# Tap weights over 128 partitions, own places for q, paired taps, a two-term third step and a new instruction order in a gated FFT-convolution and MLP kernel

## The chip, the cores and the metric

One core of a Trainium2 chip. The metric is the device time of one execution in microseconds. Engines are named as in the profile: PE (TensorE) with its weight loads PEld, DVE (VectorE), ACT (ScalarE), POOL (GpSimd), SP (SyncE, which issues the transfers).

## The reference

Inputs are 2048 tokens x 640 channels in bf16. With x = A_q:

```python
g = sigmoid((x * gate_w).sum(-1, keepdims=True))
# branch a
k_shift = sum over t of 4 taps: k shifted by t tokens * shift_k[:, t]
kv = k_shift * v
y  = irfft(rfft(kv, 2S) * rfft(ssm_k, 2S))[:S] + kv * ssm_D      # causal convolution over 2048 tokens
a  = x * y
# branch b
h  = gelu(layernorm(x) @ w1)                 # 640 -> 640
x1 = x + shift_four_channel_groups(h, +1, -1, +2, -2 tokens) @ w2
b  = x1 + gelu(layernorm(x1) @ w3) @ w4      # 640 -> 1536 -> 640
out = g * a + (1 - g) * b
```

## The kernel before

Everything is one list of 778 small tasks (`build`), each on one engine, and one order written out by hand as numbers (`ORDER`, a letter after a number puts the task on ACT, DVE or POOL). Instructions are issued in that order, so each engine runs its part as an in-order queue; `place` goes through the order once with estimated durations to choose buffers and the number of filler matmuls (`t.fill`, L255), which run on zeros while PE would idle at the start. What waits for what comes from the tasks' reads and writes.

Tokens are held as 16 tiles of 128 (token = 32 n + 16 g + s, tile s). The work in stages:

- *Head.* Transfers of x (`ldx`), w1, w2 (`ldw2a`, `ldw2b`), the convolution kernel (`ldsk`), k and v. Sine tables (TRIG, BM). For each tile of x: statistics (`st1`, L577 to L581 on DVE, L585 and L586 on ACT), 1/sqrt by a power on POOL (`rs1`, L594 to L597), normalisation (`nm1`, L601 or L631), transposes (`tr1`) and their eviction (`ev1`).
- *Branch b, first half.* `w1` (L689, L693) with gelu `g1`, `w2` (L715), `x1` (L722, adds into x and sums), squares `sq`, then `ve2` and `st2` on POOL or DVE for the second layernorm, `nm2` and transposing transfers `dt2` (L808).
- *Taps.* For four groups of four tiles (kv3, kv2, kv1, kv0), on DVE alone: four multiplications by a tap's weights (`m3` to `m0`, L878) into VC, three additions (`a2` to `a0`, L882), and the product with v (`v`, L886). The weights are loaded as one row on one partition (`ldCJ`), re-ordered there by one copy on POOL (`cjp`, 1 x 2560), written to memory (`wCJ`) and read back to all partitions (`rCJ`).
- *Convolution* by a factored Fourier transform. First step: `s1h` (L911) for the kernel and `s1x` (L913) for kv, evicted to FS and written to FH and FXD. It needs the last tap group for its last four tiles. Second step in ten blocks m: `s2h`, `s2x` (L965) and their evictions `e2` (to XH). `pa` and `pb` (L980) form the four real products on DVE, 2 x 2048 elements. Third step `s3` (L993): four terms accumulate, 32 matmuls a block:

```python
terms = [(0, 0, 0), (1, 1, 64), (0, 1, 96), (1, 0, 96)]
for n, (a, b, col) in enumerate(terms):
    for j in range(4):
        for gp in range(2):   # one matmul each
```

  `e3` evicts to GS, `wG` writes GD, `rG` reads it back into GX (four buffers), `s4` (L1031) is the last step, one tile each.
- *Branch b, second half.* `w3` (L817) in four groups of twelve with gelu `g2` (L824), `w4` (L833, L842), `t2` (L850) adds to x. The last four tiles are LATE: their w4 is cut into 512 and 128 columns.
- *End.* q is loaded again in pairs of tiles (`ldq`, two buffers in QO). `yq` (L1037) forms g * q * y on DVE into one of four places in W4's tile. `ad` (L1064) adds (1 - g) * x into one of two output buffers, for LATE tiles `ax` (L1045) and `fo` (L1051) do it in parts. `st` stores two tiles, or one for LATE.

The gate is `gate` (PE), `gz`, `gtanh`, `gg`. `dfold` adds ssm_D to the kernel's first row.

Of the kernel before, what the change touches and what calls it, by code (L numbers as in the profile page):

```python
# [31 lines left out]
WARM, COLD, PART = 7.5, 1.6, 0.95  # L32
# [5 lines left out]
41 0 23 5 29 94v 6 7 9 3 19 11 17 4 25 1 2 31 32 15 18 8 10 63v 12 13 14 26 27 87v 61a 85a 64 62 95v 104v 65v 28 42 88  # L38
86 393 24 44 96 209 43 210 55a 66v 89v 67 395 56 68a 58a 53v 54 97v 34 90a 30 399 396v 400v 57v 91 397 40 394a 93a 98
59 99v 100v 92v 60v 101 103v 143 147 16 20p 33 149 398a 102a 77a 145 79v 21 45 150 80 391 71v 72 46 22 144 148 69v  # L40
392v 82v 74a 121 39 122 450 70 78 146 107a 73v 458 35 75 451v 401p 438 37 81v 76v 439a 151 83 113v 123 36 459a 38 456
152 457a 49 84v 108 114 454 452 115v 116 125 455a 453a 110v 129 117v 446 444 126 460 118v 403 404 405 124 127 447a 162
163 406 130 128 156 157 440 105a 441a 407 159 153 154 106 160 461 47 445a 402 131 158 109a 155 442 111 132 137 443a
112a 408 161 462 466 48 138 409 463a 448 134 135 468 215p 216 449 164 140 469a 467a 119 413 141 51 221p 165 470 410 50
411 120a 166 222 223v 464 465a 167 474 471a 173 475a 174 171 217a 480 168 476 187 191 481a 482 193 477a 172 473 192
188 412 414 218 483a 478 169 195 189 170 181 415 416 417 479a 472 418 419 421 422 182 178 179 485 196 194 190 486 423
488 219a 484 225a 489a 175 220 487a 492 176 493a 136 203 424 204 494 425 490 206 498 207 495a 200 201 491a 420 426 427
428 430 502 499a 226 177 504 224 505a 211 503a 506 500 227 496 501a 239 507a 133 497 228 240 508 142 429 184 185 139
247 431 432 433 434 435 436 248 233 510 512 511a 231 513a 243 259p 509 249 514 235 234 260 232 244 515a 518 245 265p
# [34 lines left out]
class Plan:  # L84
# [13 lines left out]
    def add(self, name, eng, dur, fn, r=(), w=(), use=(), acq=(), rel=(), roles=(), after=(), mode=None, nbytes=0):  # L98
# [3 lines left out]
        t.kept = None  # L102
        t.acq = [(a, 1, a == "U") if isinstance(a, str) else a for a in acq]
# [43 lines left out]
    def place(self, order):  # L147
# [6 lines left out]
        mode, bw, flying, self.kept = None, 0.0, [], None  # L154
        start, end = [None] * n, [None] * n
        for i in order:
# [24 lines left out]
            if t.bytes:  # L181
                flying.sort()
                if len(flying) >= IN_FLIGHT:
                    at = max(at, flying.pop(0))
                start[i] = at
                free[e] = at + t.dur
                bw = max(bw, at + t.dur)
                bw += t.bytes / (HEAD_RATE if bw < HEAD else DMA_RATE)
                end[i] = bw + DMA_FIXED
                flying.append(end[i])  # L190
            else:
                d = t.dur
                if e == "PE":
# [3 lines left out]
                    if at < WARM:  # L197
                        d *= COLD
                        if self.kept is not None:
                            t.fill = int(0.95 * (at - max(free[e], 0.8)) / FILL_US[0])  # L200
                    elif self.kept is not None:
                        t.fill = max(0, int((WARM - free[e]) / FILL_US[0])) + int(PART * (at - max(free[e], WARM)) / FILL_US[1])
# [7 lines left out]
                free[e] = end[i] = at + d  # L210
            for (o, p, k) in t.rel:
# [47 lines left out]
class Env:  # L259
# [19 lines left out]
        "HT": ("H", [P, 16, D], BF16),  # L279
        "GS": ("H", [P, 10240], BF16),  # L280
# [3 lines left out]
        "XH": ("J", [P, 2, 2, 2048], BF16),  # L284
        "xn": ("L", [P, 4, D], BF16),
# [8 lines left out]
    def __init__(self, ctx, tc):  # L294
# [11 lines left out]
        self.taken = 0  # L306
# [25 lines left out]
    def early(self, name, shape, dtype):  # L332

        if name not in self.made:
# [3 lines left out]
            self.taken += n + n % 2  # L338
            v = self["C0"][0:shape[0], a:a + n]
# [15 lines left out]
def build(env, nc, io):  # L355
    pl = Plan()
    add = pl.add
    for name, n in (("U", 8), ("xn", 4), ("hs", 2), ("x1nT0", 1), ("x1nT1", 1), ("h2", 2), ("FS", 2), ("FX", 5), ("XS", 2), ("HS", 2), ("PP", 2),
                    ("GX", 4), ("Q", 2), ("O", 2), ("V", 4)):
# [51 lines left out]
    add("ident", "POOL", 0.55, c_id, r=["iotb"], w=["ID"])  # L411
# [89 lines left out]
    def c_bm(t):  # L501
        for g in range(2):
# [7 lines left out]
    dma("ldCJ", 5120, lambda t: nc.sync.dma_start(out=env["VC"][0:1, 2, :, :].rearrange("p j d -> p (j d)"),  # L510
                                                  in_=io["sk"].rearrange("d j -> (d j)").unsqueeze(0)), w=["CJR"], roles=("VC",))
    add("cjp", {"POOL": 3.2, "ACT": 2.3}, 0, lambda t: copy(t, env["VC"][0:1, 3, :, :],
                                                            env["VC"][0:1, 2, :, :].rearrange("p a b -> p (a b)").rearrange("p (d j) -> p j d", j=4)),
        r=["CJR"], w=["CJP"], roles=("VC",))
    dma("wCJ", 5120, lambda t: nc.sync.dma_start(out=env.CD[:], in_=env["VC"][0:1, 3, :, :].rearrange("p j d -> p (j d)")), r=["CJP"], w=["CD"],
        roles=("VC",))
# [56 lines left out]
    def f_st1(t, s):  # L573
        x = env["x"][:, s, :]
        if t.on == "DVE":
# [4 lines left out]
            nc.vector.tensor_scalar(out=SS("VE")[:, s:s + 1], in0=MV()[:, s, 1:2], scalar1=1e-5, scalar2=None, op0=ALU.add)  # L580
            nc.vector.tensor_scalar(out=SS("SA")[:, s:s + 1], in0=MV()[:, s, 0:1], scalar1=-1.0, scalar2=None, op0=ALU.mult)  # L581
        else:

            m = SS("SA")[:, s:s + 1]
            nc.scalar.activation(out=env["JK"][:], in_=x, func=ACT.Copy, scale=float(-1.0 / D), accum_out=m)  # L585
            nc.scalar.activation(out=env["JK"][:], in_=x, func=ACT.Square, scale=1.0, bias=m, accum_out=SS("SB")[:, s:s + 1])  # L586
# [3 lines left out]
    def f_rs1(t, s):  # L590

        c = slice(s, s + 1)
        if st1[s].on == "ACT":
            nc.gpsimd.tensor_scalar(out=SS("VE")[:, c], in0=SS("SB")[:, c], scalar1=1.0 / D, scalar2=1e-5, op0=ALU.mult, op1=ALU.add)  # L594
        nc.gpsimd.tensor_tensor(out=SS("RS")[:, c], in0=SS("VE")[:, c], in1=env.sm("MH", [P, 2])[:, 0:1], op=ALU.pow)
        if nm1[s].on == "ACT":
            nc.gpsimd.tensor_scalar(out=SS("NB")[:, c], in0=SS("SA")[:, c], scalar1=SS("RS")[:, c], scalar2=None, op0=ALU.mult)  # L597
# [21 lines left out]
    for s0 in pairs:  # L619
        nm = []  # L620
        for s in (s0, s0 + 1):
            st1[s] = add(f"st1.{s}", {"DVE": 1.26, "ACT": 1.73}, 0, lambda t, s=s: f_st1(t, s), r=[("x", s, 0), ("x", s, 1)],
                         w=[("MV", s)])
            add(f"rs1.{s}", "POOL", 0.85, lambda t, s=s: f_rs1(t, s), r=[("MV", s), "c0"], w=[("RS", s)])
        for s in (s0, s0 + 1):
            def f_nm1(t, s=s):
# [3 lines left out]
                else:  # L630
                    nc.vector.tensor_scalar(out=env["xn"][:, t.buf["xn"][0], :], in0=env["x"][:, s, :], scalar1=SS("SA")[:, c],  # L631
# [475 lines left out]
```

## Time and profile before

| | |
|---|---|
| three runs | 224.68, 225.11, 225.39 us (median 225.11) |
| the profiled execution | 227.05 us, its span 225.3 us |
| busy share of the span | PE 94%, DVE 84%, ACT 69%, POOL 20% |
| transfers | 57.94 MB, mean 257 GB/s |
| granted PE clock | 1.000 |

The span is the time from the first to the last instruction. Busy shares are means over stages of different kinds, so the stages have to be read one by one. PE's busy time holds the fillers.

### The profile page before, as it was taken

What the parts mean: (1) busy time and instruction counts of PE and PEld (TensorE: products, weight loads), DVE (VectorE), ACT (ScalarE), POOL (GpSimd) and SP (SyncE); (2) the same over time, 40 slices, a digit from 0 to 9 for tenths busy, and PEclk for the clock granted to TensorE, in tenths of its full rate; (3) what the DMA queues carried; (4) which work ended last, traced back from release to release, by engine and by line L of the source; (5) the groups of instructions that cost most, each with busy time, mean ns of one, the idle gap of its engine ahead of it and who ended that gap; (6) DMA issues with size and microseconds to landing.
All of it is one profiled execution on the core that took longest, in us unless ns stands there. A gap on an engine that the chain in (4) does not pass through costs nothing.

```text
span 225.3 us, 5381 instructions
## 1 busy us (share of the span) xinstructions
PE 212.7 (94%) x2161; PEld 106.4 (47%) x2178; DVE 189.3 (84%) x281; ACT 154.4 (69%) x225; POOL 45.8 (20%) x86
## 2 busy tenths in 40 slices
PE   3999889899999999999999999999999999999992
PEld 1576454466444444345543433334444555555561
DVE  7998896999999999997469989899857426989984
ACT  6998969799988999889658988888675002225000
POOL 7481532436200009930710000000000000000000
PEclk9999999999999999999999999999999999999999
DMA  6999999999999998979899989999992596988624
GB/s 193 281 308 232 220 237 238 327 233 327 349 240 287 241 272 252 379 270 270 193 367 311 373 154 285 316 304 309 247 255 88 185 374 209 281 250 249 203 64 116
DMA packets 39503, 57.94 MB, mean 257 GB/s; under 512 B 15027, under 2 KB 30645, under 8 KB 39478
## 3 DMA queue, kind: packets, MB, share of 16 engines
q1 hardware_dynamic: 39158, 57.27, 89.9%
q10 hardware_dynamic: 320, 0.33, 0.5%
q8 instruction: 17, 0.28, 0.5%
q14 instruction: 8, 0.07, 0.1%
HBM read 35.56 MB, written 18.36 MB: 239 GB/s over the span
## 4 chain that ended last, share of the span: by engine, by line
PE 63%; DMA 17%; DVE 12%; SPq 3%; issue 2%; ACT 1%; DVEq 0%
PE PS L817 18%; PE PS L833 17%; PE PS L715 9%; DMA x<-in_A_q_dram 7%; PE PS L965 5%; DMA W<-in_B_w_dram 4%; PE PS L689 4%; PE PS L993 4%; DMA SK<-in_A_ssm_k_dram 3%; DVE VC L878 3%; DVE VC L882 3%; DMA QO<-in_A_q_dram 2%; SPq L382 2%; PE PS L911 2%; PE PS L1031 1%
## 5 line engine op out<-in xcount | busy, mean ns | idle before, releaser
L824 ACT ACTIVATE h2T<-PS 128x512 bf16<-128x512 f32 x48 | 27.9, 605 | 27.3 <-PE PS L817 26.9
L833 PE MATMUL PS<-W,h2T 128*128 128x512 bf16 (+3 forms) x306 | 39.8, 298 | 0.3
L387 ACT CAST FS<-PS 128x1024 bf16<-128x1024 f32 x37 | 36.0, 1021 | 5.4 <-PE PS L913 3.5
L817 PEld LDWEIGHTS <-W 128*128 128x128 bf16 (+1 forms) x300 | 22.1, 103 | 29.4 <-issue 8.4
L833 PEld LDWEIGHTS <-h2T 128*128 128x128 bf16 (+1 forms) x312 | 22.4, 100 | 18.5 <-issue 1.6
L387 ACT CAST XH<-PS 128x1024 bf16<-128x1024 f32 x26 | 25.5, 1020 | 7.5 <-PE PS L965 7.4
L817 PE MATMUL PS<-x1nT,W 128*128 128x512 bf16 x120 | 28.5, 380 | 0.0
L817 PE MATMUL PS<-XB,W 128*64 128x512 bf16 (+1 forms) x180 | 28.5, 380 | 0.0
L980 DVE TENSOR_TENSOR PP<-XH 128x2048 bf16<-128x2048 bf16 x20 | 23.6, 1219 | 3.1 <-ACT XH L387 2.8
L878 DVE TENSOR_TENSOR VC<-K,VC 128x2560 bf16<-128x2560 bf16 x16 | 23.7, 1490 | 2.3 <-DMA W<-in_B_w_dram 2.1
L715 PE MATMUL PS<-W,hsT 128*128 128x128 bf16 (+1 forms) x155 | 23.5, 297 | 0.9 <-DMA W<-in_B_w_dram 0.6
L850 DVE TENSOR_TENSOR x<-PS,x 128x640 bf16<-128x640 f32 x12 | 9.8, 823 | 13.4 <-PE PS L833 13.2
L689 PE MATMUL PS<-xnT,W 128*128 128x512 bf16 x80 | 19.2, 379 | 0.1
L715 PEld LDWEIGHTS <-hsT 128*128 128x128 bf16 x160 | 12.8, 98 | 13.0 <-issue 1.1
L882 DVE TENSOR_TENSOR VC<-VC 128x2560 bf16<-128x2560 bf16 x12 | 17.9, 1489 | 0.3
L389 DVE CAST XH<-PS 128x1024 bf16<-128x1024 f32 x14 | 16.9, 1220 | 1.2 <-PE PS L965 1.1
L1037 DVE SCALAR_TENSOR_TENSOR W<-PS,GG,QO 128x640 bf16<-128x640 f32 x16 | 13.6, 877 | 2.4 <-PE PS L1031 1.9
L387 ACT CAST GS<-PS 128x1024 bf16<-128x1024 f32 x12 | 12.0, 1016 | 3.9 <-PE PS L993 3.9
L255 PE MATMUL PS<-C 128*128 128x512 bf16 x34 | 9.9, 434 | 3.8 <-DVE C L506 3.7
L842 PE MATMUL PS<-W,h2T 128*64 128x512 bf16 (+1 forms) x192 | 13.4, 299 | 0.0
L722 DVE SCALAR_TENSOR_TENSOR x<-PS,x 128x640 bf16<-128x640 f32 x16 | 12.8, 815 | 0.1
L965 PE MATMUL PS<-FX,TRIG 64*32 64x512 bf16 x320 | 12.4, 381 | 0.3 <-ACT GS L387 0.3
(115 smaller groups left out, 294.0 us busy)
## 6 DMA issues: line engine op xcount, KB each, us to landing
FH<-FS SPq DMA_DIRECT2D x8, 640.0 KB, 6.3
FXD<-FS SPq DMA_DIRECT2D x8, 640.0 KB, 5.0
FX<-FH SPq DMA_DIRECT2D x10, 512.0 KB, 6.0
FX<-FXD SPq DMA_DIRECT2D x10, 512.0 KB, 5.3
GX<-GD SPq DMA_DIRECT2D x8, 640.0 KB, 5.9
W<-in_B_w_dram SPq DMA_DIRECT2D x2, 1920.0 KB, 11.9
GD<-GS SPq DMA_DIRECT2D x8, 480.0 KB, 4.0
SK<-in_A_ssm_k_dram SPq DMA_DIRECT2D x5, 512.0 KB, 6.5
```

Of the source, the lines that this page charges most:

```text
L387: nc.scalar.copy(out=out, in_=in_)
L389: (nc.vector if t.on == "DVE" else nc.gpsimd).tensor_copy(out=out, in_=in_)
L689: nc.tensor.matmul(m[:, b, :], lhsT=W[:, 0, kb, 160 * fb:160 * fb + 128], rhs=rhs(kb, shifts[fb]), start=(kb == 0), stop=(kb == 4))
L715: nc.tensor.matmul(m[:, c0:c1], lhsT=env["hsT"][:, o.buf["hs"][0], fb, 128 * (s % 4):128 * (s % 4) + 128], rhs=env["W12"][:, 1, fb, c0:c1] ...
L817: nc.tensor.matmul(env.PS[q:q + w, t.buf["U"][0], :], lhsT=env["W3"][:, kb, 128 * fb + q:128 * fb + q + w], rhs=env.nT(int(nP[-1]))[:, :, ...
L824: nc.scalar.activation(out=env["h2T"][:, o.buf["h2"][0], fb, :], in_=env.PS[:, t.buf["U"][0], :], func=ACT.Gelu_apprx_tanh)
L833: nc.tensor.matmul(m[q:q + w, c0:c1], lhsT=env["h2T"][:, o.buf["h2"][0], fb, a:a + w], rhs=env["W4"][:, fb, c0:c1], start=(fb == 0), stop= ...
L878: nc.vector.tensor_tensor(out=VC[:, o], in0=env["K"][:, a + 3 - j:a + 7 - j, :], in1=w, op=ALU.mult)
L882: nc.vector.tensor_tensor(out=VC[:, 1], in0=VC[:, 1], in1=VC[:, 2], op=ALU.add)
L965: nc.tensor.matmul(env.U(t.buf["U"][0])[32 * j:32 * j + 32, gp, :], lhsT=CRI()[64 * gp:64 * gp + 64, 32 * pc:32 * pc + 32], rhs=X[64 * gp: ...
L980: nc.vector.tensor_tensor(out=env["PP"][:, o.buf["PP"][0], a, :].rearrange("p (b c) -> p b c", b=2), in0=X.unsqueeze(1).broadcast_to([P, 2 ...
L1037: nc.vector.scalar_tensor_tensor(out=u, in0=env.Uf(t.buf["U"][0])[:, 0:D], scalar=SS("GG")[:, s:s + 1], in1=env["QO"][:, 2 * q.buf["Q"][0] ...
```

## The change

- The tap weights are loaded as 128 partitions x 20 elements, re-ordered by one copy of that shape on DVE or ACT, and written to memory in runs of five elements; `rCJ` stays.
- Taps in pairs: one multiplication forms two taps (5120 elements) from overlapping rows of K; an addition of 5120, one of 2560, and the product with v follow. A group has five DVE instructions and not eight.
- `pa` and `pb` become one product of 4096 elements; a new task `pc` combines the products (one subtraction, one addition, 1024 elements each, DVE). Third step: two terms, 16 matmuls a block.
- Each pair of q tiles has a place of its own (five in QO, three in XH's tile, the latter after the last product). `yq` writes in place. New: `ox` on ACT scales x by (1 - g) in place, 16 of them. `ad` and `ax` become plain additions, `ad` on DVE or POOL, into x; stores read x.
- `st1` on DVE loses its last two small instructions; `rs1` on POOL always has one more. `st2` keeps only the power; its other two POOL instructions become one on DVE (`nb2`).
- `dfold`'s and `bperm`'s engines change by the order (DVE, ACT). Some early tables live in VC's tile.
- The order is new: 790 tasks. `place` knows transfers in parts, a warm-up of PE, and times in which POOL and DVE exclude each other. In the new order w2 stands 16th in SP's queue and was 22nd; x1.0 to x1.3, gz and nb2 of the first group stand ahead of taps they stood behind; all stores stand behind the last `rG`; seven `ad` are on POOL.

```diff
-    dma("ldCJ", 5120, lambda t: nc.sync.dma_start(out=env["VC"][0:1, 2, :, :].rearrange("p j d -> p (j d)"),
-                                                  in_=io["sk"].rearrange("d j -> (d j)").unsqueeze(0)), w=["CJR"], roles=("VC",))
...
+    dma("ldCJ", 5120, lambda t: nc.sync.dma_start(out=CJ()[:, 0:20], in_=io["sk"].rearrange("(p a) j -> p (a j)", a=5)), w=["CJR"], roles=("VC",))
+    add("cjp", {"DVE": 0.12, "ACT": 0.25}, 0, lambda t: copy(t, CJ()[:, 20:40].rearrange("p (j a) -> p j a", j=4), CJ()[:, 0:20].rearrange("p (a j) -> p j a", j=4)),
...
+        def taps(t, j, a=a, E=E):
+            VC, k = env["VC"], env["K"][:, a + 3 - j:a + 7 - j, :]
+            k = bass.AP(tensor=k.tensor, offset=k.offset, ap=[list(k.ap[0]), [-D, 2], [D, 4], [1, D]])
+            nc.vector.tensor_tensor(out=VC[:, 1:3] if j else E(), in0=k, in1=VC[:, 3, j:j + 2, :].unsqueeze(2).broadcast_to([P, 2, 4, D]), op=ALU.mult)
...
+        def comb(t, pa=pa):
+            PP = env["PP"][:, pa.buf["PP"][0]].rearrange("p a (b c) -> p a b c", b=2)
+            v = nc.vector if t.on == "DVE" else nc.gpsimd
+            for b, op in enumerate((ALU.subtract, ALU.add)):
+                v.tensor_tensor(out=PP[:, 0, b, :], in0=PP[:, 0, b, :], in1=PP[:, 1, 1 - b, :], op=op)
...
-            terms = [(0, 0, 0), (1, 1, 64), (0, 1, 96), (1, 0, 96)]
-            for n, (a, b, col) in enumerate(terms):
+            for n, col in enumerate((0, 96)):
...
+            def ox(t_, s=s):
+                nc.scalar.activation(out=env["x"][:, s, :], in_=env["x"][:, s, :], func=ACT.Copy, scale=SS("OG")[:, s:s + 1])
...
+            def ad(t_, s=s, i=i, u=Q):
+                x = env["x"][:, s, :]
+                (nc.vector if t_.on == "DVE" else nc.gpsimd).tensor_tensor(out=x, in0=x, in1=u(i), op=ALU.add)
```

More of the change, by code (lines that the diff above doesn't have):

```diff
@@ L116, in add @@
         return t
-    def close(self):
+    LOCKS = ("nm1.", "nm2.", "kv", "pa.", "pb.", "pc.", "ad.", "ax.", "bperm")
+    XFER = (("ldx10", 2, 0.55, 1.6), ("ldx6", 2, 0.55, 1.6), ("ldx", 2, 0.55, 0.66), ("ldkh1", 1, 0.45, 0.9), ("ldkh0", 2, 0.6, 0.6),
+            ("ldk", 2, 0.55, 1.4), ("ldv", 2, 0.55, 1.4), ("ldsk", 1, 0.45, 2.0), ("ldw1", 1, 0.45, 2.9), ("ldw2a", 1, 0.4, 1.9),
+            ("ldw2b", 1, 0.4, 0.25), ("ldw3", 1, 0.6, 5.3), ("ldw4", 1, 0.6, 5.3), ("bm", 2, 0.55, 1.5), ("rCJ", 1, 0.4, 1.9), ("ldCJ", 1, 0.4, 0.3), ("wCJ", 1, 0.4, 1.2),
+            ("wF", 1, 0.65, 1.8), ("rF", 1, 0.42, 1.4), ("rG", 1, 0.45, 1.75), ("dbt", 1, 2.4, 3.0), ("dt", 1, 1.3, 1.1), ("ldq", 2, 0.58, 0.68),
+            ("st.", 2, 0.6, 0.68))
+    def close(self):
+        for t in self.tasks:
+            if t.bytes:
+                q = next((x for x in self.XFER if t.name.startswith(x[0])), ("", 1, 0.4, max(0.1, t.bytes / 365e3)))
+                n, us = (1, 0.4) if t.name.startswith("st.") and t.bytes < 250000 else (q[1], q[3])
+                t.parts = [(q[2], us)] * n
+        for t in self.tasks:
+            t.lock, t.hold = t.name.startswith(self.LOCKS), t.name in ("cjp", "dfold", "bz") or t.name[:3] == "ad."
+            t.steps = {"rs": 1, "ve": 2, "st": 0}.get(t.name[:2], 0)
+            t.gelu = t.name.startswith(("g1.", "g2."))
         by_role = {}
@@ L181, in place @@
             if t.bytes:
-                flying.sort()
-                if len(flying) >= IN_FLIGHT:
+                for k, (issue, us) in enumerate(t.parts):
                     at = max(at, flying.pop(0))
[L185 to L190, printed above, removed]
-            else:
-                d = t.dur
+                    if k == 0:
+                        start[i] = at
+                    at += issue
+                    bw = max(bw, at) + us
+                    flying.append(bw + DMA_FIXED)
+                free[e], end[i] = at, bw + DMA_FIXED
+            else:
+                if t.lock and e == "DVE" and held[0] <= at < held[1]:
+                    start[i] = at = held[1]
+                more = 0.0
+                if e == "POOL" and at < locked[1]:
+                    if at >= locked[0]:
+                        start[i] = at = locked[1]
+                        more = 1.5 * t.steps if locked[2] else 0.0
+                    elif t.hold and at + t.dur > locked[0]:
+                        more = 3.0
+                        free["DVE"] += 3.0
+                d = t.dur + more
                 if e == "PE":
@@ L210, in place @@
                 free[e] = end[i] = at + d
+                if t.gelu and not gelu:
+                    gelu = True
+                    free[e] = end[i] = at + d + TABLE
+                if t.hold and e == "POOL":
+                    held = (at, end[i])
+                if t.lock and e == "DVE":
+                    locked = (at, end[i], t.name[:2] == "kv")
             for (o, p, k) in t.rel:
@@ L999, in ev3 @@
                 copy(t_, env["GS"][:, a:a + 1024], env.Uf(t.buf["U"][2 * h]))
[L1000 removed]
+            add(f"e3.{m}.{h}", {"ACT": 1.03, "DVE": 1.23}, 0, ev3, use=[t], rel=[(t, "U", 2 * h), (t, "U", 2 * h + 1)], w=[("GS", m % 5, h)], after=("HT", "EH"), roles=("GS",))
         i = m % 5
```

218 lines of the change are left out of this document (99 added, 119 removed), and 5 rows, old and new, of the table ORDER.

## Prediction

> **What bounds the kernel now.** I read the page first, then busy time by stretch with the cuts at turns of the chain of waits, then the waits of TensorE and VectorE, then the chain.
>
> ```profile
> span 225.3 us, 5381 instructions
> PE 212.7 (94%) x2161; PEld 106.4 (47%) x2178; DVE 189.3 (84%) x281; ACT 154.4 (69%) x225; POOL 45.8 (20%) x86
> ...
> 0.00:40.63 40.63, 33.71 (x287) 19.17 (x291) 34.58 (x98) 35.10 (x53) 18.77 (x44) 1.00 0.94 248
> 40.63:101.33 60.70, 60.16 (x434) 29.10 (x442) 59.44 (x72) 53.55 (x81) 22.02 (x27) 1.00 1.01 287
> 101.33:114.47 13.14, 13.09 (x103) 7.36 (x112) 7.17 (x16) 9.18 (x19) 5.01 (x15) 1.00 0.97 251
> 114.47:174.00 59.53, 58.94 (x831) 23.79 (x834) 51.96 (x50) 48.62 (x61) 0.00 (x0) 1.00 0.96 271
> 174.00:187.08 13.08, 12.97 (x95) 7.32 (x98) 4.43 (x5) 1.01 (x1) 0.00 (x0) 1.00 0.78 287
> 187.08:220.87 33.79, 33.78 (x426) 19.68 (x424) 30.66 (x40) 6.94 (x12) 0.00 (x0) 1.00 0.68 197
> 220.87:225.30 4.43, 0.00 (x0) 0.00 (x0) 1.05 (x3) 0.00 (x0) 0.00 (x0) 1.00 0.54 148
> ...
> L255 PE MATMUL PS<-C 128*128 128x512 bf16 x34 | 9.9, 434 | 3.8 <-DVE C L506 3.7
> ...
> 30.95 9.63 DMA W<-in_B_w_dram
> ...
> 96.30 1.49 DVE K L886
> ...
> 99.67 1.23 DVE FS L389
> ...
> 100.93 0.39 PE PS L913 x2
> 101.33 6.84 PE PS L833 x49
> ```
>
> In the stretch rows the columns are the length, then busy time of PE, weight loads, DVE, ACT and POOL, then clock, DMA share, GB/s. Two things stand there. From 40.63 to 220.87 TensorE is idle for 180.24 - 178.94 = 1.3 us, so every TensorE microsecond removed there can count. And before 40.63 it does little: 33.71 us less 9.9 us of fillers (L255), 23.8 of 40.63 us, so 16.8 us are lost, until w2 lands. But between 40.63 and 101.33 VectorE is as full (59.44 of 60.70), and the chain runs through it: the last tap group's product (L886) ends at 97.79, and only then come the last first-step products (L913), which end at 101.33. So the first 101 us have two bounds, TensorE and VectorE's queue of taps; the rest has one, TensorE. Only 4.43 us follow its last matmul.
>
> The execution in the profile took 227.05 us, 1.75 more than its span; the runs have a median of 225.11. I forecast the change of the span and apply it to that median.
>
> **Head and taps.** The new order puts w2's main load at place 16 of SP's queue, where it was 22nd, after x, w1 and two of five ssm_k blocks. Ahead of it and with it go about 5.3 MB instead of 9.4. At the first stretch's 248 GB/s 9.4 MB are 37.9 us, and it landed at 40.58, 2.7 later; 5.3 MB give 21.4 + 2.7 = 24 us. TensorE then finds first-layer and second-layer work some 10 us earlier, and a good part of the 16.8 lost us can go. That doesn't shorten anything by itself: the last first-step products still wait for the last tap group, so VectorE's queue up to there has to be counted.
>
> ```profile
> L878 DVE TENSOR_TENSOR VC<-K,VC 128x2560 bf16<-128x2560 bf16 x16 | 23.7, 1490 | 2.3 <-DMA W<-in_B_w_dram 2.1
> L980 DVE TENSOR_TENSOR PP<-XH 128x2048 bf16<-128x2048 bf16 x20 | 23.6, 1219 | 3.1 <-ACT XH L387 2.8
> ...
> 58.00 1.49 DVE L878 TENSOR_TENSOR VC<-K,VC 128x2560 bf16<-128x2560 bf16 x1
> 59.52 1.49 DVE L882 TENSOR_TENSOR VC<-VC 128x2560 bf16<-128x2560 bf16 x1
> ...
> L581 DVE TENSOR_SCALAR SA<-MV 128x1 f32<-128x1 f32 x10 | 1.4, 144 | 0.0
> L722 DVE SCALAR_TENSOR_TENSOR x<-PS,x 128x640 bf16<-128x640 f32 x16 | 12.8, 815 | 0.1
> L603 DVE TENSOR_SCALAR xn<-x,r,SB 128x640 bf16<-128x640 bf16 x10 | 4.3, 437 | 0.4 <-POOL SB L787 0.4
> ...
> 99.31 0.09 DVE xn L603
> ...
> 51.23 1.36 PE PS L715 x10
> ...
> L389 DVE COPY xnT<-PS 128x1280 bf16<-128x1280 bf16 (+2 forms) x6 | 4.1, 702 | 0.1
> ```
>
> L878 and L980 are the same operation at 2560 and 2048 elements: 271 ns for 512 more, 0.529 ns an element. A pair of taps (5120) then takes 1490 + 1355 = 2845 ns. A group goes from 8 instructions at a pitch of 1.52 us (59.52 less 58.00), 12.2 us, to three of 2.88 and two of 1.52, 11.7 us; four groups save 2.0. Two 144 ns instructions leave each of 10 statistics: at most 2.9, and since short ones overlap I take 1.3. x1.14 and x1.15 go behind the taps: 2 x 0.815, 1.6. What comes ahead of the last tap: one eviction more (the FS cast above, 1.23), three normalisations more (3 x 0.437 = 1.3), one eviction of xnT (0.7), gz (from 97.79 to 99.31, 1.5), and dfold, cjp and two small nb2, about 0.6. Sum 5.3 against 4.9: 0.4 us more, before waits. The taps stand at position 56 of VectorE's queue, not 44, so x1.0 to x1.3 are ahead of them and they wait for w2's landing too; w2 at 24 us is in time, if ScalarE's activations are. I take VectorE's idle time there as it was: the last product ends at 98.2. After it TensorE has five first-step products; w2.12 (1.36 us, the L715 row), which stood among them, is earlier now; I count 1.1 of it, since the products also wait for evictions. 101.33 + 0.4 - 1.1 is 100.6, **0.7 us earlier**. The ends: 4.5 us earlier still if most of VectorE's waits of the first 40 us go (40.63 - 34.58 = 6.0), 7 later if first-layer work arrives late.
>
> The tap weights themselves: ldCJ, wCJ and rCJ are SP's as before; the re-ordering copy is 128 lanes x 20 elements on VectorE, counted above. wCJ waits for it in SP's queue with ldsk4, ldk15 and rCJ behind; x1.0 is ahead of that copy, so these loads can't be issued before about 29 us. The taps want them at about 44, after 15 us, and ldk's landings take 9.5 us:
>
> ```profile
> K<-in_A_k_dram SPq DMA_DIRECT2D x8, 320.0 KB, 9.5
> ```
>
> I cost it at nothing; if that cover goes, the taps slip one for one. The Trainium skill, "DMA: Bandwidth & Descriptors" (Specifications), says that transfers below 512 B miss line rate by a read-modify-write, and wCJ now writes runs of 10 B; no row before prices that, and by it the slip would be part of the 7 us above.
>
> **Step three.** Two of four terms are dropped, and VectorE combines the products.
>
> ```profile
> L993 PE MATMUL PS<-PP,TRIG 32*64 32x512 bf16 x320 | 10.5, 379 | 0.1
> ...
> 173.00 1.00 PE PS L993 x32
> ...
> L389 DVE CAST XH<-PS 128x1024 bf16<-128x1024 f32 x14 | 16.9, 1220 | 1.2 <-PE PS L965 1.1
> L387 ACT CAST XH<-PS 128x1024 bf16<-128x1024 f32 x26 | 25.5, 1020 | 7.5 <-PE PS L965 7.4
> L601 ACT ACTIVATE xn<-x,NB,RS 128x640 bf16<-128x640 bf16 x4 | 3.6, 916 | 0.0
> ...
> 187.81 2.16 PE PS L817 x20
> ```
>
> 32 matmuls take 1.00 us; 16 take 0.50; ten times: **5.0 us less on TensorE**. VectorE: one product of 4096 elements is 1219 + 1084 = 2.30 us in place of 2.44, and two combining instructions of 1024 are 0.68 each, 1.35: 1.2 more per block, 12.1 in all. Does that fit? In 114.47:174.00 TensorE spends 59.53; minus 5.0, plus two more w4 (3.3 each; they come before the last third step in the new order; two are 6.84 in the chain's row at 101.33) and two w3.3 (1.1 each, two are 2.16) gives 63.3. VectorE: 51.96 + 12.1, two evictions less (2.4), three t2 more (2.4, as L722), 1.1 less in small things: 63.0. ScalarE: 48.62 + 2 evictions (2.0) + four ox (3.7, by the 916 ns row) + two nm2 (1.8): 56.1. So VectorE, which had 7.6 us of slack, has none: 63.0 against 63.3. Before, with slack, TensorE lost 0.59 there. Bounds for the new stalls: 0, and 5 (the whole saving). I take 1.5, nearer to the old 0.59.
>
> **End.** Each q block has a place of its own, so q loads no longer wait for buffers, and sums go in place into x.
>
> ```profile
> 163.56 12.25 SPq L1005 DMA_DIRECT2D GD<-GS  x5
> 178.80 9.37 SPq L1019 DMA_DIRECT2D GX<-GD  x5
> ...
> 187.08 0.73 PE L1031 MATMUL PS<-GX,BT 128*64 128x512 bf16 x8
> ...
> GX<-GD SPq DMA_DIRECT2D x8, 640.0 KB, 5.9
> ...
> L1064 DVE SCALAR_TENSOR_TENSOR QO<-x,OG,W 128x640 bf16<-128x640 bf16 x12 | 10.0, 878 | 0.3 <-DMA out_dram<-QO 0.3
> L865 POOL TENSOR_TENSOR HT<-HT,C 1x640 bf16<-1x640 bf16 x1 | 1.4, 1415 | 0.4 <-DVE HT L389 0.4
> ```
>
> From the last third step (174.00) to the first G load's issue are 4.8 us, to its landing 10.7. The old order covers that with four w4, 13.1 us; the new with two w4 and four w3.3, 10.9. That leaves 0.2, and s4.10 has 4.6 us between its buffer's release and its use against a landing of 5.9: I add 0.2 for both, 2 as the upper bound. The sums: sixteen scaled additions of 0.88 become plain ones of 1219 - 1408 x 0.529 = 0.47, nine of them on VectorE and seven on GpSimd, where the one comparable row (640 elements) has 1.4; ScalarE gets sixteen ox of 0.92, and it was busy 6.94 of the last 33.79 us. So VectorE gains some 10 us there (16 x 0.88 less 9 x 0.47) and TensorE stays the bound; the wait for q was beside it. The last addition now follows a 128-column piece with another store already issued: VectorE ended 1.05 us after TensorE, it will end about 0.4 after: **0.65 less**.
>
> GpSimd's additions meet VectorE:
>
> ```profile
> 57.56 0.19 POOL L775 TENSOR_TENSOR v<-S 128x2 f32<-128x2 f32 x1
> ...
> 88.68 1.54 POOL L775 TENSOR_TENSOR v<-S 128x2 f32<-128x2 f32 x1
> ```
>
> The same instruction takes 0.19 us between taps and 1.54, a tap's length, beside one. Longer pairs make such waits up to 2.85; they sit on statistics needed much later, 0 us. The Trainium skill, "SBUF — State Buffer" (Who interferes with whom), has it as an exclusive lock: whichever starts first keeps the other out for a whole instruction. By that rule, the trace agrees for GpSimd's side; its other side, VectorE held by an addition, speaks against the change and is a rival below.
>
> Sum: -0.7 - 5.0 + 1.5 + 0.2 - 0.65 = -4.65; 225.11 - 4.65 = **220.5 us**.
>
> **Rivals.** *The head pays too.* VectorE's early waits shrink by 4.5: 216.0. For: w2 at 24 us; 16.8 lost us. Against: 56 tasks ahead of the taps, about 40 us long by their rows. 0.18. *The saving turns into VectorE's bound*: in-order queues with 63.0 against 63.3 lose 3 more: 223.5. For: no slack; against: 0.59 lost so far. 0.17. The same with 4.5 lost is no change, 225.0: 0.06. *GpSimd holds VectorE*: seven additions of 1.4, each after waiting for a VectorE instruction of 0.9, are 16 us in a queue; st.8 waits for the last, and st.14 and st.12 stand behind it on SP: 1.5 later, 222.0. Against: the last G products for it come 10 us before TensorE's end. 0.05. *Slower: taps late.* If w2.0 to w2.3 or the tap weights arrive so that the first pair starts at 52 instead of 44, the last product ends at 106, everything behind slips by 8: 228.5. It decides from 4.7 us of slip on. For: four x1 and the re-ordering copy now stand ahead of the taps; against: DMA lead of 15 us. 0.14. The forecast keeps 0.40.
>
> **Numbers.** A measurement here tells about 0.3% (0.7 us) from no change. Faster: 0.40 + 0.18 + 0.17 + 0.05 = 0.80; same 0.06; slower 0.14. The range takes the head's case with 1.5 below it and the balance case with 2.5 above: 214.5 to 226.0; left out is most of the slower case and the far end of the first.
>
> **What would show it.** w2 landing near 24 us; first pair near 44, 2.85 each; the last L886-like product near 98; third steps of 0.50; TensorE idle by 1 to 3 us in the two-term stretch with VectorE over 95% there; no q wait at the end; 3.8 us behind the last matmul. A first pair after 49 makes the forecast wrong upward, a last product before 95 downward.

## Result and the profile after

The changed kernel takes 232.44 us (median of 4, 232.26 to 234.47) against 225.25 (224.68 to 225.71): a ratio of 1.034, 95% interval 1.028 to 1.040. It is 7.2 us slower where 4.65 less was forecast. Executions more than 1.5% above the fastest of their kernel are left out of all ratios below (two of four with four terms back and two of four with the fillers, which have no ratio for that), and the one profile that was taken in such an execution, with the sums on GpSimd again, isn't read. Times below are medians of all executions, except where two single times are named; ratios are to the kernel before, run beside each experiment on the same chip. A stretch or a wait is from the one execution in the profile.

The page of the kernel after, and its busy time by stretch, cut at the same turns as in the prediction (length, busy PE, weight loads, DVE, ACT, POOL, then clock, DMA share, GB/s):

```profile
span 230.8 us, 5076 instructions
PE 214.4 (93%) x2018; PEld 105.1 (46%) x2018; DVE 187.5 (81%) x253; ACT 168.9 (73%) x244; POOL 48.8 (21%) x91
...
0.00:47.47 47.47, 41.95 (x348) 23.79 (x349) 35.77 (x93) 39.89 (x64) 19.90 (x63) 1.00 0.83 217
47.47:104.07 56.60, 53.65 (x385) 24.96 (x384) 55.91 (x52) 45.30 (x68) 15.85 (x14) 1.00 1.00 291
...
117.17:184.71 67.54, 65.70 (x742) 26.07 (x742) 61.86 (x58) 56.34 (x71) 0.00 (x0) 1.00 0.90 257
184.71:195.61 10.90, 10.90 (x90) 5.92 (x90) 2.87 (x3) 3.31 (x5) 0.00 (x0) 1.00 0.83 266
195.61:226.92 31.31, 29.15 (x366) 17.09 (x362) 25.28 (x33) 12.09 (x19) 10.23 (x7) 0.95 0.71 209
226.92:230.80 3.88, 0.00 (x0) 0.00 (x0) 0.35 (x1) 0.00 (x0) 0.00 (x0) 1.00 0.54 141
```

TensorE still has its 214 us of work (212.7 before), but over a longer span. Against the prediction's own steps: first tap pair at 47.47 (forecast 44), end of the first step 104.07 (100.6), two-term stretch 67.54 (63.3 + 1.5), last third step to last matmul 42.21 (38.3: 13.08 + 33.79 - 8.8 + 0.2), behind it 3.88 (3.8). The three large misses are +3.5, +2.7 and +3.9. Each has lines of its own.

First miss: the chain of waits ahead of the taps (start, length, what; pieces under 0.1 us are left out, but for the copy VC), what VectorE waited for there, and the transfers in that time:

```profile
28.32 0.83 DVE x L737 x2
29.15 0.09 DVE VC L405
29.27 4.13 DMA CD<-VC
33.41 0.33 SPq L532
33.79 0.72 SPq L398
34.56 12.83 DMA K<-in_A_k_dram
...
38.88 1.22 DVE L405 COPY HT<-PS 128x2048 bf16<-128x2048 bf16 x1 [2.17 <-PE PS L875]
...
47.47 2.83 DVE L898 TENSOR_TENSOR VC<-K,VC 128x5120 bf16<-128x5120 bf16 x1 [3.20 <-DMA K<-in_A_k_dram]
```

```profile
28.90:34.60 5.70, 5.70 (x72) 4.66 (x71) 5.19 (x15) 4.43 (x11) 2.36 (x8) 1.00 0.38 27
```

The re-ordering copy of the tap weights (VC) stands behind x1.0 on VectorE; wCJ, the store of the copy, waits for it in SP's queue; rCJ, which reads it back, waits 4.13 us for the store; and two blocks of k (ldk11, ldk7) stand behind rCJ. From 28.9 to 34.6 the transfers move 27 GB/s. Part of that is the queue that stands still; but ldsk4 and ldk15 went out between 29.69 and 31.37 and hardly moved either, and why isn't shown. Then four loads of k go out at once, and what the first pair needs lands after 12.83 us. VectorE sits idle for it for 3.20 us: it is done with the instruction ahead of the pair at 44.27, where the forecast has the pair at 44.

Second miss: TensorE's groups of the third step (L993, now L1020) and of the second (L965, now L987), before and then after, and one third step from the chain after:

```profile
L993 PE MATMUL PS<-PP,TRIG 32*64 32x512 bf16 x320 | 10.5, 379 | 0.1
L965 PE MATMUL PS<-FX,TRIG 64*32 64x512 bf16 x320 | 12.4, 381 | 0.3 <-ACT GS L387 0.3
...
L1020 PE MATMUL PS<-PP,TRIG 32*64 32x512 bf16 x160 | 7.2, 387 | 0.3 <-DVE XH L405 0.2
L987 PE MATMUL PS<-FX,TRIG 64*32 64x512 bf16 x320 | 13.1, 382 | 1.3 <-ACT GS L403 0.5 <-DMA FX<-FH 0.3 <-DVE XH L405 0.2
...
126.00 0.57 PE PS L1020 x16
```

Half the matmuls of the third step (160 for 320) bring 10.5 us of busy time down to 7.2, not to 5.3.

Third miss, TensorE's waits, and the stretches behind the longest of them:

```profile
PE PS L1060 <- DMA GX<-GD: 2.2, 1, 2.2
```

```profile
209.80:212.00 2.20, 2.16 (x38) 1.71 (x40) 1.66 (x2) 1.05 (x2) 0.00 (x0) 0.71 0.18 70
212.00:214.00 2.00, 2.00 (x14) 0.84 (x12) 1.83 (x4) 0.00 (x0) 0.79 (x1) 0.50 0.02 4
214.00:216.00 2.00, 2.00 (x22) 1.10 (x20) 1.96 (x3) 0.00 (x0) 2.00 (x2) 0.97 0.04 10
```

Before block 10's fourth step TensorE waits 2.2 us for its G load, and right behind it the granted clock is 0.71, 0.50, 0.97. What the clock withholds there is 2.20 x 0.29 + 2.00 x 0.50 + 2.00 x 0.03 = 1.7 us.

### The profile page after: what moved, and what is told of

Read it like the earlier page. It is cut to its first block, busy times and chain, and to the rows that moved or that the text cites. A ratio compares the mean times of both kernels' runs of the same rounds, so it can differ in the third digit from the quotient of the medians.

```text
span 230.8 us, 5076 instructions
## 1 busy us (share of the span) xinstructions
PE 214.4 (93%) x2018; PEld 105.1 (46%) x2018; DVE 187.5 (81%) x253; ACT 168.9 (73%) x244; POOL 48.8 (21%) x91
## 4 chain that ended last, share of the span: by engine, by line
PE 36%; DVE 26%; DMA 21%; ACT 6%; issue 6%; SPq 3%; DVEq 0%; ACTq 0%
PE PS L833 10%; PE PS L849 9%; DVE VC L903 7%; PE PS L858 6%; DMA K<-in_A_k_dram 6%; DMA x<-in_A_q_dram 5%; DVE VC L898 4%; DVE x L737 4%; DMA FX<-FH 3%; DVE XH L405 3%; PE PS L730 3%; DMA GX<-GD 3%; DMA GD<-GS 3%; PE PS L987 2%; DVE PP L1002 2%
## 5 line engine op out<-in xcount | busy, mean ns | idle before, releaser
L403 ACT CAST FS<-PS 128x1024 bf16<-128x1024 f32 x37 | 35.6, 1024 | 7.9 <-PE PS L932 2.9
L840 ACT ACTIVATE h2T<-PS 128x512 bf16<-128x512 f32 x48 | 28.0, 608 | 12.9 <-PE PS L833 12.4
L1096 POOL TENSOR_TENSOR x<-x,QO 128x640 bf16<-128x640 bf16 x6 | 8.8, 1478 | 90.6 <-ACT x L1071 86.9
L403 ACT CAST XH<-PS 128x1024 bf16<-128x1024 f32 x23 | 22.9, 1020 | 5.0 <-PE PS L987 4.9
L730 PE MATMUL PS<-W,hsT 128*128 128x512 bf16 (+1 forms) x160 | 23.6, 299 | 1.8 <-DVE x L737 1.8
L1002 DVE TENSOR_TENSOR PP<-XH 128x4096 bf16<-128x4096 bf16 x10 | 22.9, 2288 | 1.9 <-ACT XH L403 1.4
L403 ACT CAST GS<-PS 128x1024 bf16<-128x1024 f32 x18 | 17.9, 1023 | 5.2 <-PE PS L1020 3.0
L405 DVE CAST XH<-PS 128x1024 bf16<-128x1024 f32 x17 | 20.5, 1218 | 1.2 <-PE PS L987 1.0
L742 ACT ACTIVATE JK<-x 128x640 bf16<-128x640 bf16 x16 | 11.8, 740 | 5.5 <-DVE x L737 5.1
L858 PE MATMUL PS<-W,h2T 128*64 128x128 bf16 (+1 forms) x192 | 15.3, 319 | 0.0
L987 PE MATMUL PS<-FX,TRIG 64*32 64x512 bf16 x320 | 13.1, 382 | 1.3 <-ACT GS L403 0.5
L898 DVE TENSOR_TENSOR VC<-K,VC 128x5120 bf16<-128x5120 bf16 x4 | 11.3, 2820 | 3.2 <-DMA K<-in_A_k_dram 3.2
L1071 ACT ACTIVATE x<-x,OG 128x640 bf16<-128x640 bf16 x16 | 12.7, 828 | 1.5 <-DVE x L866 1.5
```

The costliest lines, as they stand in the source:

```text
L403: nc.scalar.copy(out=out, in_=in_)
L405: (nc.vector if t.on == "DVE" else nc.gpsimd).tensor_copy(out=out, in_=in_)
L730: nc.tensor.matmul(m[:, c0:c1], lhsT=env["hsT"][:, o.buf["hs"][0], fb, 128 * (s % 4):128 * (s % 4) + 128], rhs=env["W12"][:, 1, fb, c0:c1] ...
L840: nc.scalar.activation(out=env["h2T"][:, o.buf["h2"][0], fb, :], in_=env.PS[:, t.buf["U"][0], :], func=ACT.Gelu_apprx_tanh)
L858: nc.tensor.matmul(env.PS[q:q + w, t.buf["U"][0], 0:c1 - c0], lhsT=env["h2T"][:, o.buf["h2"][0], fb, a:a + w], rhs=env["W4"][:, fb, c0:c1] ...
L898: nc.vector.tensor_tensor(out=VC[:, 1:3] if j else E(), in0=k, in1=VC[:, 3, j:j + 2, :].unsqueeze(2).broadcast_to([P, 2, 4, D]), op=ALU.mult)
```

## Experiments

Orders are shown by task names, and only what moves. In each, the rest is the kernel after unless said otherwise.

**Early weights.**

```diff
- SP: ldw2b3 ... ldw2a ldCJ ... wCJ ldsk4 ldk15 rCJ ldk11 ldk7     DVE: cjp behind x1.0
+ SP: ldCJ ldw2b3 ... ldw2a ... wCJ ldsk4 ldk15 ldk11 ldk7 rCJ     DVE: cjp before st1.6
```

> The changed kernel with the tap weights' chain moved in the order alone: ldCJ and cjp ahead of the last four statistics of VectorE, rCJ behind the three loads of k that it stood in front of. Theory A (the taps are late because SP's queue stands at wCJ, 24.5 to 29.3, and at rCJ, 31.4 to 33.4, with the loads of k behind): the k landing that the first pair waits for comes 5 to 7 us earlier, the first pair starts by 44.5 and not at 47.5, the last tap product ends at 97 to 98.5 and not 101.4, and the time falls by 3 to 4.5 us from 232.4 to 228 to 229.5. Theory B (from 117 on VectorE and ScalarE bound the two-term stretch, and what comes early is eaten there): the taps come early, the last third step does not, the time falls by under 1.5 us.

228.19 us, ratio 1.014 (1.007 to 1.020): 2.0% less than after, 4.5 us. SP's queue no longer stands still ahead of the loads, and the pair starts at 41.14:

```profile
23.39 0.39 SPq L530 DMA_DIRECT2D CD<-VC  x1
23.82 0.50 SPq L567 DMA_DIRECT2D SK<-in_A_ssm_k_dram  x1
24.37 4.70 SPq L398 DMA_DIRECT2D K<-in_A_k_dram  x6
29.99 0.33 SPq L532 DMA_DIRECT2D VC<-CD  x1
...
41.14 2.81 DVE L898 TENSOR_TENSOR VC<-K,VC 128x5120 bf16<-128x5120 bf16 x1
```

That is 6.3 us earlier, more than the 3.20 that VectorE sat idle for k: ldsk4 too stood behind wCJ, and VectorE's 2.17 us of waiting for what comes of it (at 38.88 above) are 0.17 here. The last tap product ends at 95.5 instead of 101.4. One microsecond is given back behind the first step, where w4's weights now come late (the wait of TensorE for W is 1.0).

**The two-term step alone**, in the kernel before and its order.

```diff
  pb: second product of the block
+     PP[0,b] = PP[0,b] -/+ PP[1,1-b]   (two instructions of 1024 elements)
- s3: for a, b, col in (0,0,0) (1,1,64) (0,1,96) (1,0,96)
+ s3: for n, col in (0, 96): rhs = PP[0,n]
```

> The kernel before with the two-term third step alone (VectorE combines the two products after the second of them, order as before). Theory B (VectorE has no room for 13.5 us more): TensorE's third steps fall from 1.00 to 0.57 us, but the stretch from the first second step to the last third step stays at 59.5 us or grows by up to 4; time 225 to 229. Theory A (the two-term step is good and only the head and the end spoil the change): the stretch falls by 3 to 4.3 us, time 221 to 222.

232.94, ratio 1.036 (1.031 to 1.040). Alone, the step that should save most costs 7.8 us:

```profile
113.89:179.79 65.90, 57.80 (x671) 22.24 (x673) 63.14 (x70) 48.73 (x61) 0.00 (x0) 1.00 0.83 244
...
PE PS L817 <- DVE GS L389: 2.2, 4, 1.1
```

The stretch goes from 59.5 to 65.9 with VectorE at 63.14, 96%: in the old order the saving does turn into VectorE's bound, and TensorE waits for VectorE's evictions.

**Four terms back in the kernel after**, without the combining.

```diff
- pc: PP[0,b] = PP[0,b] -/+ PP[1,1-b]
- s3: for n, col in (0, 96): rhs = PP[0,n]
+ s3: for a, b, col in (0,0,0) (1,1,64) (0,1,96) (1,0,96)
```

> The changed kernel with the four-term third step back (no combining instructions on VectorE, 32 matmuls a block, same order). Theory B: VectorE's slack is back (61.9 busy of 67.5 us becomes about 48), TensorE gets 4.3 us of work and loses 3.3 us of stalls: time 232 to 234. Theory A: the stretch grows by the whole 4.3 us, time 236 to 237.

232.33 and 233.83 us, no interval. In the profile (of 233.83) the stretch is 69.3 instead of 67.5, so there the step is worth 1.8 us in the new order as given. Of that 1.2 is left in the span (232.0 for 230.8): the end is 1.3 shorter (40.9), with a G wait of 1.8 us and the clock behind it at 1.00, but what follows the last matmul is 0.8 longer (4.7). The two times alone don't tell it from nothing.

**No combining**: VectorE has 20 instructions less.

```diff
- pc: PP[0,b] = PP[0,b] -/+ PP[1,1-b]
+ pc: nothing
```

> The changed kernel without the subtraction and addition that combine the products (left out: 20 instructions of 0.68 us on VectorE, so the third step works on two uncombined products); TensorE does what it did. Theory B (VectorE bounds the stretch of 67.5 us, where it is busy 61.9): the stretch falls to 64 to 65, time 229 to 230. Rival B2 (ScalarE, with 56.3 busy, or the transfers of the second step bound it): the stretch stays above 66.5, time 231.5 or more.

231.32, ratio 1.021 (1.012 to 1.030).

```profile
114.21:181.11 66.90, 64.85 (x742) 25.84 (x742) 49.65 (x38) 56.24 (x71) 0.00 (x0) 1.00 0.96 264
```

With 12 us less on VectorE the stretch shortens by 0.6 only. So VectorE doesn't bound it in the new order; TensorE's own 64.85 us fill it. The time is 1.3% below after, with intervals that overlap.

**w4 first in the end**, two pieces of late w4 ahead of block 10's fourth step, to cover the G load.

```diff
- PE: w3.3.8 w4.8 s4.10 s4.13 w4.13.1 s4.11 w4.15.0
+ PE: w3.3.8 w4.8 w4.13.1 w4.15.0 s4.10 s4.13 s4.11          ACT: g2.3.11 g2.3.8 behind w3.3.8
```

> The changed kernel with w4.13.1 and w4.15.0 (3.3 us of TensorE work) moved ahead of s4.10 and s4.13 in the order. Theory C (TensorE waits 2.2 us for the G load of s4.10, after which its granted clock is 0.71, 0.50 and 0.97 for 6 us): no wait there, clock 1.00, the stretch from the last third step to the last matmul falls from 42.3 to 38.5 us, time 228 to 229. Rival (the end is bound by VectorE's sums and the stores, which come as late in any case): under 1 us.

234.32, ratio 1.038 (1.032 to 1.044): not faster. The G wait is gone, and another takes its place, now on VectorE, with the same clock behind it:

```profile
PE PS L858 <- DVE x L1083: 1.9, 1, 1.9
...
213.00:217.00 4.00, 2.08 (x12) 1.07 (x13) 3.96 (x5) 0.00 (x0) 3.11 (x2) 0.67 0.31 75
217.00:221.00 4.00, 4.00 (x29) 2.40 (x27) 3.06 (x6) 0.00 (x0) 1.11 (x1) 0.50 0.72 175
```

**Fillers in the wait**: eight matmuls ahead of block 10's fourth step, whose result is written over.

```diff
  s4.10:
+     8 x matmul(U, BT[0:64], W4[0:512])
      matmul(U, BT, GX) ...
```

> The changed kernel with eight matmuls on data at hand in front of those of s4.10, into the bank that s4.10 overwrites; they fill some 1.8 us of TensorE's wait for the G load. Theory C1 (the wait costs twice: 2.2 us of itself, and 1.9 us through the clock of 0.71 and 0.50 granted behind it): the clock stays at 1.00 from 200 us on, the 192 matmuls of the last w4 take about 13.4 us and not 15.3, time 230.5 from 232.4. Theory C2 (the clock falls for another reason, or VectorE's sums bound the end): under 0.7 us.

231.58 and 229.99, no interval. In its profile the clock at the end stays at 1.00, and last third step to last matmul is 40.8 instead of 42.2. That fits the clock's part, but what follows the last matmul is 4.9 instead of 3.9, so 0.4 of the 1.4 us is left. (In the head of the same execution the clock did fall; see the last section.) The two times alone decide nothing.

**Early weights and block 2 beside block 3**, so that block 10's buffer comes free earlier.

```diff
- PE: s4.3 s4.7 w3.3.11 s4.2 s4.6
+ PE: s4.3 s4.2 w3.3.11 s4.7 s4.6        (products and sums of the blocks likewise)
```

> The kernel with the weights early (228.2), and s4.2 in the order right behind s4.3 (s4.7 takes its old place), so that the buffer of the G load for s4.10 is free 1.6 us earlier. Theory C: the load is issued and lands 1.6 us earlier, TensorE's wait of 1.0 us before s4.10 goes, time 227 to 227.4. Rival (VectorE's sums bound the end, as the wait on fo in the run with w4 moved ahead says): the wait goes, the time stays within 0.5 us of 228.2.

227.57, ratio 1.010 (1.003 to 1.017). Against early weights alone no difference can be told. The load goes out some 1.1 us earlier, but it takes longer to land, as the transfers are full, and TensorE still waits 1.6 us for it:

```profile
PE PS L1060 <- DMA GX<-GD: 1.6, 1, 1.6
...
201.50:204.00 2.50, 1.39 (x32) 0.92 (x28) 1.19 (x2) 1.00 (x3) 1.39 (x2) 1.00 0.97 249
```

**All sums on VectorE.**

```diff
- POOL: ad.4 ad.2 ad.1 ad.11 ad.6 ad.9 ad.8
+ DVE:  the same seven, at the same places
```

> The changed kernel with its seven GpSimd additions of the end on VectorE, at the same places of the order. Lock theory (GpSimd's additions of 1.48 us keep VectorE waiting: some of its 0.49 us additions took 0.9 to 1.3 us in the groups): the end gets shorter by 0.5 to 2 us. Rival (VectorE has no room there, seven times 0.41 us is 2.9 us more in its queue): longer by 0.5 to 3 us. Neither on the path: within 0.5 us of 232.4.

230.58, ratio 1.024 (1.017 to 1.031): 1.0% less than after, with intervals that overlap. Its profile has a G wait of 1.1 us instead of 2.2 and a clock of 1.00 behind it, so this doesn't say that the sums themselves cost anything.

**Block 13 first.** Its load is issued ahead of block 10's.

```diff
- PE: w4.8 s4.10 s4.13 w4.13.1 s4.11
+ PE: w4.8 s4.13 w4.13.1 s4.10 s4.11     DVE: yq.13 yq.10     ACT: g2.3.11 g2.3.8 behind w3.3.8
```

> The kernel after, with one thing moved on TensorE: block 13's fourth step and its w4 piece go ahead of block 10's fourth step (the load of block 12/13 is issued before that of 10/11). Theory D: the 2.2 us wait before block 10 is the landing of the third G load in a row on full DMA queues, and the granted clock of 0.71 and 0.50 behind it is that wait's doing; with 1.9 us of work put into it the wait falls under 0.5, the clock stays at 1.00, and of the 2.2 + 1.9 us between 3 and 4 come back: 228.4 to 229.4. Rival: the wait only moves (to block 13's own load, or to VectorE, as when w4 went first): from last third step to last matmul still 42, time 231.5 to 233. A third outcome, wait gone but clock still falling, would be 230 to 230.5.

231.0, ratio 1.0245 (1.021 to 1.028): 1.0% less than after, about 2 us, half of what was expected. The wait shrinks to 1.0 and the clock stays at 1.00, but the order costs something elsewhere: 0.5 us of waiting for VectorE's sums, and 5.0 us behind the last matmul instead of 3.9.

**Put together**: early weights and sums on VectorE; then block 13 first as well; then the first G store too.

```diff
- SP: wG.1 rFx.6 ldq.4 rFx.8 ldq.8 rFh.7 wG.0
+ SP: wG.1 wG.0 rFx.6 ldq.4 rFx.8 ldq.8 rFh.7
```

> The kernel after with the tap weights' chain early (which gave 4.25 us) and with all sums on VectorE (which gave 1.9 us alone). If the two costs lie in different places (taps ahead of the first step; GpSimd's sums at the end) they add: 226.3. Rival: with the taps early the end is bound by the same G loads anyway and the sums give nothing: 228.2.

> The kernel before this one and block 13 first. If all three causes are separate: 226.3 less 1 to 2.5 (the wait was 1.0 to 1.1 in either kernel alone, and their clock fell less): 224 to 225.3, level with the kernel before (225.2). Rival, block 13's place gives nothing once the sums are on VectorE: 226.3.

> The one before, with the first G store moved ahead of three q loads and two step-two loads in SP's queue, so that ScalarE's eviction of the fourth block need not wait 2.3 us for its buffer. If that wait holds up the two-term stretch: stretch 66 to 66.5 instead of 67.3, time 0.7 to 1.2 lower than the one before. Rival: TensorE lost only 0.5 us to ScalarE's G evictions, its own content bounds the stretch: no difference over 0.5 us.

227.70, 226.95 and 226.77; ratios 1.010 (1.005 to 1.015), 1.006 (1.003 to 1.009), 1.004 (1.001 to 1.008). Early weights and sums don't add: the first is level with early weights alone. The third's stretch is 66.58 where the second's is 67.47, and ScalarE's G evictions no longer hold TensorE (0.9 us there), but its time can't be told from the second's.

**Sums on GpSimd again, four terms, and a repeat**, each from that last kernel.

> Weights early, block 13 first, first G store early (the kernel with 226.77), but the seven sums on GpSimd as in the kernel after. Theory E: the last 15 us of those kernels are VectorE's (chain of waits through its sums and products), so seven sums less there (7 x 0.48 = 3.4 us) give up to 1.5 us: 225.3 to 226.3, and 3.9 to 4.5 us behind the last matmul instead of 5.2. Rival (GpSimd and VectorE keep each other out): VectorE's remaining sums stretch from 0.49 to 0.9 and more, and the time is 227 to 228.5, with a new TensorE wait for VectorE over 1 us.

> The kernel with 226.77, with four terms in the third step and no combining. Theory F: each third step costs TensorE 1.00 instead of 0.57, ten times 4.3 us, less what VectorE's 10.9 us fewer let go (about 1 by the run without combining): 3 us more, 229.5 to 230, stretch near 69.5. Rival: the stretch is bound by round trips through evictions, and four terms cost 1 us or less, as with the order as given: 226.8 to 227.8, stretch 67.5.

> The kernel with 226.77 once more, on the same chip as the two others: 226.8, stretch 66.6, about 1.004 of the kernel before.

With the sums on GpSimd 226.64, 1.003 (1.000 to 1.007); the repeat 226.77, 1.003 (0.999 to 1.007): where the sums are done makes no difference here. The time lies between those of the two theories, and no profile says which of their mechanisms is at work. Four terms: 229.04, 1.014 (1.009 to 1.019), 1.1% or 2.5 us more than the repeat. So once most waits around it are gone, the two-term step is worth 2.5 us. The stretch of four terms, then the repeat from that stretch to the end:

```profile
114.21:183.52 69.31, 68.48 (x898) 28.49 (x902) 49.83 (x38) 56.34 (x71) 0.00 (x0) 1.00 0.84 241
```

```profile
112.59:179.10 66.51, 65.19 (x739) 26.07 (x742) 61.69 (x58) 56.26 (x71) 0.00 (x0) 1.00 0.91 257
179.10:189.99 10.89, 10.84 (x88) 5.91 (x90) 2.88 (x3) 3.31 (x5) 0.00 (x0) 1.00 0.84 273
189.99:218.56 28.57, 27.85 (x366) 18.17 (x362) 24.71 (x40) 12.10 (x19) 0.00 (x0) 1.00 0.74 222
218.56:223.30 4.74, 0.01 (x1) 0.00 (x0) 0.35 (x1) 0.00 (x0) 0.00 (x0) 0.98 0.56 144
```

No version beat the kernel before; the best are level with it.

## Why the prediction was wrong

**The tap weights, costed at nothing.** This is the first failed step, worth 3.5 us at the first step's end and 4.5 in the time. The prediction saw that wCJ waits in SP's queue for the copy on VectorE, and set a landing of 9.5 us against 15 us of cover. It missed that the first pair needs a second block of k (ldk11), which stands behind rCJ as well, so that the copy, the store's landing (4.13) and k's landing (12.83, not the 9.5 of the median row before) come one after the other: 29.15 + 0.12 + 4.13 + 1.16 for the issues + 12.83 = 47.4. The named rival, taps late, has the right mechanism but said that it decides from 4.7 us of slip; with 3.5 us it decided nothing alone. Early weights, which change the order of that queue and of the copy alone, give 4.5 us, so the queue is shown as the cause. (They also free ldsk4, which is why they give more than the 3.5.) What was right: w2 in time, pairs of 2.82 (2.85 forecast), and taps that keep VectorE full from there.

**Step three, -5.0 on TensorE.** This term was mis-sized: halving the row of 1.00 us ignored a part that doesn't halve. Start to start a third step alone took about 1.00 before and takes 0.57 now, 4.3 saved in ten, and by the busy sums above 3.3. So 1.7 of the 2.7 is here, and 0.7 is step two's matmuls (13.1 for 12.4). The new stalls were about right in size: TensorE is idle for 1.84 us in the stretch, 0.59 before, where 1.5 more was set. Some 0.6 us stays open. The cause named for the stalls was wrong: VectorE was busy 61.9 of 67.5 us, 92%, not over 95, and without its combining the stretch hardly moves. Freed of most waits around it, the step measured 2.5 us in the time. In the old order, the rival "VectorE's bound" is what happens, with more than its price: +7.8.

**The end, +0.2.** It cost 3.9. The wait itself (2.2) went just over the bound of 2 for the G loads' round trip, and a stall of TensorE there had a price behind it that the prediction didn't have: the clock, 1.7 by the sum above. Block 13 first took away half of the wait and all of the clock's part. But that isn't all, for the second step that failed here is "TensorE stays the bound": what follows the last matmul grows when the stretch before it shrinks. From the last third step to the end of the span the kernel after takes 46.1 us, the fillers 45.7, block 13 first 45.3, and the repeat, with a G wait of 0.2 and the clock at 1.00, still 44.2; the forecast's terms give 42.1. So about half of the miss stays when wait and clock are gone. Nor is the clock's loss in every execution of the kernel after: one with a mean granted clock of 0.999, so at most some 0.2 us withheld, took 232.33 us, about as long as the profiled one (0.993, 232.54). In the kernel after the chain at the end is TensorE's; in most of the other runs it passes through VectorE, for 3.9 us in the repeat (pieces under 0.3 us are left out):

```profile
197.49 6.05 DMA GX<-GD
203.58 0.48 PE PS L1060 x4
204.14 1.69 DVE QJ L1066 x2
205.92 1.30 DVE x L1096 x3
207.21 0.41 DVE QJ L1077
207.65 0.36 DVE x L1083
208.05 3.45 PE PS L858 x48
```

**Tail, -0.65.** Measured 3.88 behind the last matmul, 0.55 less than before; right in the kernel after, but not a property of the change: the faster variants have 4.7 to 5.5, for the reason just given.

**GpSimd.** Its sums take 1.48 us (1.4 forecast), and VectorE's take 1.53 where they start beside them, 0.48 alone:

```profile
203.33 4.36 POOL L1096 TENSOR_TENSOR x<-x,QO 128x640 bf16<-128x640 bf16 x3 [86.89 <-ACT x L1071]
...
204.90 1.53 DVE L1096 TENSOR_TENSOR x<-x,QO 128x640 bf16<-128x640 bf16 x1
212.99 0.48 DVE L1096 TENSOR_TENSOR x<-x,QJ 128x640 bf16<-128x640 bf16 x1
```

So the lock holds VectorE too, as the rival had it, and the trace agrees there with the rule of the Trainium skill that the prediction cites. The waiting hides behind other work, since moving the sums changed nothing in the kernel put right.

**The base.** The profiled execution of before took 227.05, 1.9 above its median, and that of after 232.54, at its median. So a span that comes out 10.2 us over the forecast (3.5 + 2.7 + 3.9 + 0.1) is 11.9 in the medians. Where the 1.9 us lay in before's execution isn't settled. In the repeat's profile (an execution of 225.09, 1.7 below its median) the same steps miss the forecast by little: the two-term stretch starts 1.2 us earlier (112.59 for 113.7) and is 1.7 longer, the end is 1.2 and what follows it 1.0 longer. Also open is why the G wait was 1.1 with the sums on VectorE and 2.2 with them on GpSimd: the loads' issues stand alike, their landings differ.

## What to carry to other kernels

Follow a moved transfer through its in-order queue: ask what stands behind each instruction that waits for a computed value, and put loads that depend on nothing ahead of it. Work that goes from a full engine to one with slack paid here only when the order around it was made anew: the same two-term step was +7.8 us in the old order, -1.8 in the stretch of the new one and -2.5 when the waits around it were gone. Half the matmuls of a group need not take half its time: 0.57 us for 1.00 here. And read the end as a whole, past the last matmul: a wait that is taken away there came back in part behind it.

## What was not expected of the hardware

TensorE's granted clock at the end stays at 1.00 behind G waits of 1.0 to 1.8 us in seven of these kernels (1.8 with four terms back, 1.6 with block 2 beside block 3), and is at 0.50 for 2 to 5 us behind 1.9 (w4 first) and 2.2 us (after). But the length of the wait doesn't decide. A wait of 2.07 us in the head of the kernel after left the clock at 1.00. At one and the same place, the wait for a block of ssm_k, 1.91 us with the fillers brought 0.50 and 2.24 us with the sums on VectorE left it at 1.00 (from 36 to 44). And with four terms in the last kernel, 1.21 us of waiting for w4's weights, with two waits of 0.35 ahead of it, brought 0.50. The fillers, the sums on VectorE, then four terms:

```profile
36.63 1.91 PE L875 MATMUL PS<-ID,SK 128*128 128x128 bf16 x16 [1.91 <-DMA SK<-in_A_ssm_k_dram]
...
38.00:40.00 2.00, 2.00 (x10) 0.92 (x8) 1.34 (x2) 0.57 (x1) 0.00 (x0) 0.50 0.94 248
...
37.00 1.21 PE L875 MATMUL PS<-ID,SK 128*128 128x128 bf16 x16 [2.24 <-DMA SK<-in_A_ssm_k_dram]
...
99.61 0.61 PE L849 MATMUL PS<-W,h2T 128*128 128x512 bf16 x1 [1.21 <-DMA W<-in_B_w_dram]
...
100.00:102.00 2.00, 1.78 (x5) 0.76 (x5) 0.65 (x2) 1.97 (x5) 0.00 (x0) 0.50 1.53 271
```

What is withheld is the same each time, some 1.7 us: 1.7 in the kernel after, 2 x (0.32 + 0.50 + 0.04) = 1.7 with the fillers (36 to 42), 2 x (0.21 + 0.50 + 0.15) = 1.7 with four terms (98 to 104), and about twice that, 4 x (0.33 + 0.50) = 3.3, with w4 first. What decides whether a wait brings it is open.

The Trainium skill, "TensorE: Matmul & The Clock Gate" (HAM oscillation — how this bites in real kernels), warns of idle gaps over some 3.4 us and of a half clock behind them; the half clock agrees with the 0.50 here, but shorter gaps (1.2 to 2.2 us) brought it. And the store of the tap weights, 5 KB in runs of 10 B, took 4.13 us to land while the transfers moved 27 GB/s, about as long as the stores of 480 KB (GD<-GS, 3.8 in the page's issues).
